# One scale for the whole spatial matrix, from row tiles, in place of one per half from transposed blocks

## The chip, the core and the metric

The kernel runs on one core of a Trainium2 chip. The metric is the device time of one execution in microseconds (us). The kernel before was run three times: 777.92, 780.03 and 781.29 us, with a median of 780.03 us. One further execution was recorded by the hardware profiler; the profile and the trace below are of that one.

A core has five engines that run side by side, each with its own queue of instructions, worked through in order: TensorE (PE, matrix products), VectorE (DVE), ScalarE (ACT), GpSimd (POOL) and SyncE (SP, which here only issues transfers). They wait for one another through semaphores. TensorE writes its results into PSUM, eight banks of [128 x 512] float32; everything else lies in the on-chip memory SBUF, 128 partitions of 207 KB in this kernel, or in device memory.

## The reference

Two blocks follow each other on a sequence of T = 2048 tokens of width D = 1024: a memory-augmented attention with 32 heads, and a gated MLP. The change lies wholly in the second.

```python
def _B_ref(x, w_in, w_sp, b_sp, w_out):     # x: layernorm of h, [1, 2048, 1024]
    z = _gelu(jnp.einsum('bsd,df->bsf', x, w_in))          # w_in [1024, 3584]
    z1 = z[..., :Fh].copy()                                # Fh = 1792
    z2 = _layernorm(z[..., Fh:], axis=-1)
    g = jnp.einsum('ts,bsf->btf', w_sp, z2) + b_sp[None, :, None]   # w_sp [2048, 2048]
    return jnp.einsum('bsf,fd->bsd', z1 * g, w_out)        # w_out [1792, 1024]

h = x + _A_ref(_layernorm(x), ...)
h2 = h + _B_ref(_layernorm(h), ...)
```

All tensors are bfloat16. The spatial matrix `w_sp` mixes tokens: its product with z2 is the gate of z1.

## The kernel before, in words

**A recorder sets the waits.** Each engine's instructions are recorded in the order in which the program issues them. Class `_Recorder` derives the waits from the memory that each instruction reads and writes, in cells of 32 bytes of SBUF and whole banks of PSUM. Each engine then runs its own list in order, so an instruction that waits holds everything behind it on its engine. Since `run` emits every instruction at line 210, the profile gives L210 for nearly all of them, and groups are told apart by the names of their tiles.

**Stages.** First comes the attention (0 to about 310 us), whose output h is written to `out`. Then comes the *z2 half* (to about 404 us): `z2_group(k, tc)` multiplies a row tile of 128 tokens by 448 columns of `w_in` in eight matmuls, and ScalarE's Gelu takes the result from PSUM to `Z2`. There are 4 x 16 such groups, in the order of the list `todo`; a few of them run inside the attention already, and a few output tiles of the attention are mixed in. `z2_stats` and `z2_apply` on VectorE, with two small instructions on GpSimd (`zrs`), normalise the rows into `Z2H` (float16). SyncE loads the column pieces of `w_in` (`win_load`) and transposes the normalised h (`hnT`).

The *z1 half* follows (about 404 to 501 us): for s = 0 to 3 (512 tokens each) and fc = 0 to 13 (128 features each), eight matmuls give a block of z1 transposed, and a Gelu on ScalarE stores it in `Z1T`. Beside it the first half of `w_sp` is prepared.

**The gate in two halves.** The gate is computed for output tokens 0 to 1023 (pr = 0) and then 1024 to 2047 (pr = 1). In each half, `w_sp` is seen as four blocks of 512 x 1024 (`b11`, `b12`, `b21`, `b22`), loaded transposed by SyncE (`sp_load`, four transposing transfers a block), and a Strassen-like scheme uses their sums t1 to t4 and sums of blocks of z2 (`s_sum`, tile `SS`), with seven products of eight matmuls for each of seven groups of features (`gate_group`). The blocks and sums are float16. Since the values of `w_sp` are small, they are first multiplied by a power of two:

```python
def sp_half(pr, k):
    dve.tensor_single_scalar(BH[k][:], RAW[k][:], SC[pr][:], ALU.mult)
```

The power of two comes from the root mean square of the entries: `sp_square` squares half a block on ScalarE and adds up each partition's squares in a column of `SQ` (eight columns), and `sp_scale` copies these to bfloat16 on GpSimd (`SQB`), sums over the partitions with a matmul against a matrix of ones (`ONES`), and makes the scale `SC` and its inverse `INV` in a few tiny instructions on VectorE and one on GpSimd. The inverse is applied in `gate_group`. Scale and inverse exist once for each half pr.

**Between the two gate halves lie the output units.** Each of the 16 units in the loop at line 1110 is a product of 14 matmuls for 128 tokens by 512 columns (`out_unit`); VectorE adds it to the part of h that was loaded back from `out` (`fin`), and ScalarE's queue issues the write. The load of `fin` for unit n + 2 and the write of unit n are both issued from ScalarE's queue, in that order, with four `fin` buffers. While the units run, the second half of `w_sp` is loaded and squared (n = 1 to 8, line 1115), scaled (n = 8, line 1118) and summed (n = 8 to 12), so that the second gate stage can begin. A last stage of 17 output units ends the kernel.

**Banks.** `next_bank` hands out the eight banks of PSUM in turn, in the z2 half, the z1 half, the gate and the output units alike. A group that takes a bank must wait until its previous content was read, eight groups earlier.

**Memory around the change.** `RAW` and `BH` of a block share their place: the scaling is in place. `t3` overwrites `b12`, `t1` takes the place of a dead activation tile. The squares write to a scratch tile `SJ` that nothing reads.

Of the kernel before, what the change touches and what calls it, by code (L numbers as in the profile page):

```python
# [12 lines left out]
T = 2048  # L13
# [245 lines left out]
def bass_sequential_preLN__memory_aug_infini_attn__mixer_gmlp__prompt_kernel(  # L259
# [24 lines left out]
    def tens(name, shape, dt, off):  # L284
        sz = int(np.prod(shape[1:])) * mybir.dt.size(dt)
        assert off % 32 == 0 and off + sz <= ARENA, (name, off, sz)
        t = nc.alloc_sbuf_tensor_at(name, list(shape), dt, offset=abase + off)
        R.space[t[:].tensor.name] = ("sbuf", off)
        return t

    class Bump:
# [4 lines left out]
        def __call__(self, name, shape, dt):  # L296
# [72 lines left out]
          for k, o in ROLES + (("t1", 30), ("t2", 190), ("t3", 22), ("t4", 38))}  # L369
# [4 lines left out]
    ZRS = b3("zrs", [128, NTC], F32)  # L374
    ONES = b3("ones", [128, 128], BF16)
    MHZ = b3("mhz", [128, 1], F32)
    SQ = b3("sq", [128, 8], F32)
    SQB = b3("sqb", [128, 8], BF16)
    TOT = b3("tot", [128, 1], F32)
    TOP = b3("top", [128, 1], F32)  # L380
    SC = [b3("sc%d" % i, [128, 1], F32) for i in range(2)]
    INV = [b3("inv%d" % i, [128, 1], F32) for i in range(2)]
    TMP = {k: tens("tmp_" + k, [128, L], F32, (4 + 2 * i) * K)
           for i, k in enumerate(("s1", "s1b1", "s1b2", "u2", "u3"))}
    SJ = [tens("sj0", [128, 4, L], BF16, 4 * K), tens("sj1", [128, 4, L], BF16, 38 * K)]
    BROW = [tens("brow%d" % i, [128, L], BF16, (132 + i) * K) for i in range(2)]
    WO0 = tens("w_out0", [128, 14, 512], BF16, 118 * K)
    WO1A = tens("w_out1a", [128, 7, 512], BF16, 54 * K)
# [15 lines left out]
    def next_bank():  # L404
        b = rot["banks"][rot["n"] % len(rot["banks"])]
        rot["n"] += 1
        return b
# [390 lines left out]
    def z2_group(k, tc, stage=None):  # L798
        s, tcl = divmod(tc, 4)
        b = next_bank()  # L800
        wi = WIN[k % 3]
        mm8(PS[:, b, 0:448], lambda i: HNT[s][:, i, tcl * 128:(tcl + 1) * 128], lambda i: wi[:, i, 0:448])
        if stage is None:
            z2_gelu(k, tc, PS[:, b, 0:448])
        else:
            act.activation(ZSTG[stage][:], PS[:, b, 0:448], ACTF.Copy)
            staged.append((k, tc, ZSTG[stage][:]))
# [99 lines left out]
    rot["n"] = 0  # L907
    win_load(2)

    todo = [(0, 2), (0, 3), (0, 8), (0, 9), 0, (0, 10), 1, (0, 11), 2, (1, 0), 3]  # L910
    todo += [(1, tc) for tc in range(1, 4)] + [(0, tc) for tc in range(12, NTC)]
    todo += [(1, tc) for tc in range(4, NTC)] + [(k, tc) for k in (2, 3) for tc in range(NTC)]
    for it in todo:
        if isinstance(it, int):
            for half in range(2):
                wo(NSEG - 1, it, half)
                bg_pop()
            continue
        z2_group(*it)
        bg_pop()  # L920
        z2_stats()
        if len(zs) > 1:
            z2_stats()
        if len(zq) > 1:
            z2_apply()
        if it == (0, NTC - 1):
            win_load(3)
        if it == (1, NTC - 1):
            for k in (4, 6, 7):
                win_load(k)  # L930
        if it == (2, NTC - 1):
            win_load(5)
    assert not any(lnq)
    while zs:
        z2_stats()
    pool.memset(ONES[:], 1.0)
    pool.memset(MHZ[:], -0.5)

    def sp_load(pr, k, j):
        r0, c0 = 1024 * pr + (512 if k in ("b12", "b22") else 0), 1024 if k in ("b21", "b22") else 0  # L940
        sp.dma_start_transpose(RAW[k][:, :, j * 128:(j + 1) * 128],
                               B_w_sp[r0 + j * 128:r0 + (j + 1) * 128, c0:c0 + 1024])

    def sp_square(pr, k, h):
        col = 2 * [x for x, _ in ROLES].index(k) + h
        act.activation(SJ[pr][:], RAW[k][:, 4 * h:4 * h + 4, :], ACTF.Square, accum_out=SQ[:, col:col + 1])

    def sp_scale(pr):
        b = next_bank()
        pool.tensor_copy(SQB[:], SQ[:])  # L950
        pe.matmul(PS[:, b, 0:8], ONES[:], SQB[:], start=True, stop=True)
        dve.tensor_reduce(out=TOT[:], in_=PS[:, b, 0:8], axis=mybir.AxisListType.X, op=ALU.add)
        dve.tensor_single_scalar(TOT[:], TOT[:], 1e-30, ALU.max)
        pool.tensor_tensor(TOP[:], TOT[:], MHZ[:], ALU.pow)
        dve.tensor_single_scalar(TOP[:].bitcast(I32), TOP[:].bitcast(I32), 0x7F800000, ALU.bitwise_and)
        dve.tensor_single_scalar(SC[pr][:], TOP[:], 8192.0, ALU.mult)
        dve.reciprocal(INV[pr][:], SC[pr][:])

    def sp_half(pr, k):
        dve.tensor_single_scalar(BH[k][:], RAW[k][:], SC[pr][:], ALU.mult)  # L960

    def sp_sum(o, a, b):
        dve.tensor_tensor(BH[o][:], BH[a][:], BH[b][:], ALU.subtract)
# [25 lines left out]
    def gate_group(pr, g, ba):  # L989
        t1, t2 = slice(1024 * pr, 1024 * pr + 512), slice(1024 * pr + 512, 1024 * pr + 1024)  # L990
        s1, s1b1, s1b2, u2, u3 = (TMP[k][:] for k in ("s1", "s1b1", "s1b2", "u2", "u3"))
        inv = INV[pr][:]

        def stt(o, b, add):
            dve.scalar_tensor_tensor(o, bank(b), inv, add, ALU.mult, ALU.add)

        def out(v, i, t):
            z = Z1T[:, g + 7 * i, t]
            dve.tensor_tensor(z, v, z, ALU.mult)

        act.activation(s1, bank(ba), ACTF.Copy, scale=inv)
        pool.tensor_tensor(s1b2, s1, BROW[1][:], ALU.add)
        pool.tensor_tensor(s1b1, s1, BROW[0][:], ALU.add)
        bb, bc = next_bank(), next_bank()
        prod(bb, SS[:, 1], "t2", True)
        prod(bc, SS[:, 0], "t1", True)
        stt(u2, bb, s1b2)
        if pr == 0 and g == 0:
            sp_sum("t4", "b21", "t2")
        if g < 6:  # L1010
            s_sum(1, g + 1)
        prod(bb, SS[:, 2], "t3", False)
        prod(ba, a_blk(0, 1, g), "b21", False)
        stt(u3, bb, s1b2)
        stt(u3, bc, u3)
        out(u3, 1, t2)
        nb = prod1(g + 1) if g < 6 else None
        if g < 6:
            s_sum(3, g + 1)
        stt(s1, ba, BROW[0][:])  # L1020
        out(s1, 0, t1)
        prod(bc, SS[:, 3], "b22", False)
        if g < 6:
            s_sum(2, g + 1)
        prod(bb, a_blk(1, 1, g), "t4", False)
        stt(u2, bc, u2)
        out(u2, 0, t2)
        if g < 6:
            s_sum(4, g + 1)
        stt(s1b1, bb, s1b1)  # L1030
        out(s1b1, 1, t1)
        return nb
# [28 lines left out]
    for s in range(NSEG):  # L1061
        for fc in range(14):
            k, fl = divmod(fc, 4)
            b = next_bank()
            mm8(bank(b), lambda i: WIZ[k][:, i, fl * 128:(fl + 1) * 128], lambda i: HNT[s][:, i, :])
            act.activation(Z1T[:, fc, s * 512:(s + 1) * 512], bank(b), ACTF.Gelu_apprx_tanh)
            if zq:
                z2_apply()
            if s == 1 and fc in (2, 4, 6, 8):
                sp_square(0, "b11" if fc > 4 else "b21", fc // 2 % 2)  # L1070
            if s == 1 and fc in (10, 12) or s == 2 and fc in (8, 10):
                sp_square(0, "b22" if s == 1 else "b12", fc // 2 % 2)
            if s == 2 and fc == 13:
                sp_scale(0)
            if s == 3:
                if fc < 4:
                    sp_half(0, ("b11", "b12", "b22", "b21")[fc])
                if fc == 4:
                    sp_sum("t1", "b12", "b11")
                if fc == 5:  # L1080
                    s_sum(1, 0)
                    s_sum(2, 0)
                    s_sum(3, 0)
                    s_sum(4, 0)
                if fc == 6:
                    sp_sum("t3", "b22", "b12")
                if fc == 8:
                    sp_sum("t2", "b22", "t1")
        if s == 0:
            for j in range(4):  # L1090
                sp_load(0, "b22", j)
        if s == 1:
            for j in range(4):
                sp_load(0, "b12", j)
            brow_load(0)
# [5 lines left out]
        nb = gate_group(0, g, nb)  # L1101
    fin_load(units[0], act)
    fin_load(units[1], act)
    for k in ("b11", "b21", "b12", "b22"):
        for j in range(4):
            sp_load(1, k, j)
    brow_load(1)
# [2 lines left out]
    for n, u in enumerate(units):  # L1110
        if n + 2 < 16:
            fin_load(units[n + 2], act)
        out_unit(u, (lambda i: WO0[:, i, :]) if u[1] == 0 else
                 (lambda i: WO1A[:, i, :] if i < 7 else WO1B[:, i - 7, :]), act)
        if 0 < n < 9:
            k = (n - 1) // 2
            sp_square(1, ("b11", "b21", "b12", "b22")[k], (n - 1) % 2)
        if n == 8:
            sp_scale(1)
            sp_half(1, "b11")  # L1120
            sp_half(1, "b12")
        if n == 9:
            sp_sum("t1", "b12", "b11")
            sp_half(1, "b22")
        if n == 10:
            sp_sum("t3", "b22", "b12")
        if n == 11:
            sp_sum("t2", "b22", "t1")
        if n == 12:
            sp_half(1, "b21")  # L1130
            sp_sum("t4", "b21", "t2")
        if n == 13:
            for k in range(1, 5):
                s_sum(k, 0)
# [44 lines left out]
```

## Time and profile before

| what | value |
|---|---|
| median of three runs | 780.03 us (777.92 to 781.29) |
| profiled execution | 781.06 us |
| its span, first to last instruction | 779.3 us |
| mean granted TensorE clock | 0.995 |
| PE busy | 765.2 us (98%) |
| DVE busy | 465.6 us (60%) |
| ACT busy | 336.6 us (43%) |
| POOL busy | 201.4 us (26%) |
| read from device memory, written | 34.35 MB, 8.39 MB |
| chain that ended last, by engine | PE 91%, DMA 3%, DVE 3%, ACT 1%, issue 1% |

The page gives each engine's busy time and its share of the span, then the span in 40 equal slices of 19.5 us with one digit each (tenths of busy time; 9 is 90% or more). PEclk is the granted TensorE clock in tenths of full speed. An engine with a share near 100% sets the time; the idle time of the others costs nothing by itself. A list of waits names who released an engine from each wait. The chain that ended last follows the work back from the last instruction, at each step to what released it.

### The profile page before, as it was taken

What the parts mean: (1) busy time and instruction counts of PE and PEld (TensorE: products, weight loads), DVE (VectorE), ACT (ScalarE), POOL (GpSimd) and SP (SyncE); (2) the same over time, 40 slices, a digit from 0 to 9 for tenths busy, and PEclk for the clock granted to TensorE, in tenths of its full rate; (3) what the DMA queues carried; (4) which work ended last, traced back from release to release, by engine and by line L of the source; (5) the groups of instructions that cost most, each with busy time, mean ns of one, the idle gap of its engine ahead of it and who ended that gap; (6) DMA issues with size and microseconds to landing.
All of it is one profiled execution on the core that took longest, in us unless ns stands there. A gap on an engine that the chain in (4) does not pass through costs nothing.

```text
span 779.3 us, 13105 instructions
## 1 busy us (share of the span) xinstructions
PE 765.2 (98%) x5477; PEld 368.4 (47%) x5552; DVE 465.6 (60%) x851; ACT 336.6 (43%) x395; POOL 201.4 (26%) x363
## 2 busy tenths in 40 slices
PE   8999999999999999999999999999999799999998
PEld 4445544555554445455554444444444244444444
DVE  5585689768954775744464004397873386878422
ACT  6777876887778676133333755300002500000000
POOL 2564556555553342100132000112110002112000
PEclk9999999999999999999999999999999899999999
DMA  9654555353425423724311330110039840000122
GB/s 306 162 149 89 95 82 123 82 96 83 101 50 130 105 67 62 202 61 136 96 36 32 55 67 1 55 41 0 1 55 251 161 155 15 1 1 0 61 82 74
DMA packets 131595, 66.66 MB, mean 86 GB/s; under 512 B 95952, under 2 KB 124368, under 8 KB 131536
## 3 DMA queue, kind: packets, MB, share of 16 engines
q1 hardware_dynamic: 124288, 59.01, 32.2%
q10 hardware_dynamic: 7248, 6.82, 3.2%
q8 instruction: 43, 0.70, 0.4%
q14 instruction: 16, 0.13, 0.1%
HBM read 34.35 MB, written 8.39 MB: 55 GB/s over the span
## 4 chain that ended last, share of the span: by engine, by line
PE 91%; DMA 3%; DVE 3%; ACT 1%; issue 1%; ACTq 0%; POOL 0%; DVEq 0%
PE ps L210 91%; DMA out_dram<-fin 2%; DMA wv<-in_A_wv_dram 1%; ACT sj L210 1%; DVE stats L210 1%; ACTq L210 0%; DVE hch L210 0%; DVE pqk L210 0%; DVE otok L210 0%; DVE ta L210 0%; ACT e L210 0%; DVE fin L210 0%; DVE lno L210 0%; ACT L210 0%; DVE rd L210 0%
## 5 line engine op out<-in xcount | busy, mean ns | idle before, releaser
L210 ACT ACTIVATE e<-ps 128x2048 bf16<-128x2048 f32 (+1 forms) x96 | 152.6, 1590 | 41.7 <-PE ps L210 41.5
L210 POOL TENSOR_SCALAR_AFFINE_SELECT e<-e 128x512 bf16<-128x512 bf16 x128 | 90.8, 722 | 131.9 <-ACT e L210 131.9
L210 PE MATMUL ps<-win,hnT 128*128 128x448 bf16 x512 | 98.3, 352 | 0.0
L210 PE MATMUL ps<-hnT,wiz 128*128 128x512 bf16 x439 | 96.2, 379 | 0.5
L210 ACT ACTIVATE tmp_s<-ps,inv 128x512 f32<-128x512 f32 x14 | 9.6, 687 | 159.0 <-DVE z1T L210 131.6
L210 POOL TENSOR_TENSOR tmp_s1b<-tmp_s,brow 128x512 f32<-128x512 f32 x28 | 32.3, 1157 | 168.5 <-ACT tmp_s L210 137.1
L210 PEld LDWEIGHTS ps<-win,hnT 128*128 128x128 bf16 x512 | 49.7, 98 | 46.4 <-issue 0.2
L210 PEld LDWEIGHTS ps<-hnT,wiz 128*128 128x128 bf16 x448 | 43.7, 98 | 52.7
L210 ACT ACTIVATE z<-ps 128x448 bf16<-128x448 f32 x60 | 32.5, 543 | 69.4 <-PE ps L210 69.4
L210 PE MATMUL ps<-xnT,wk 128*128 128x512 bf16 x233 | 59.6, 380 | 1.2
L210 PE MATMUL ps<-wv,xnT 128*128 128x512 bf16 x255 | 59.8, 382 | 0.8 <-DMA wv<-in_A_wv_dram 0.7
L210 DVE TENSOR_TENSOR fin<-fin,ps 128x512 bf16<-128x512 bf16 (+2 forms) x33 | 22.1, 671 | 60.3 <-PE ps L210 42.6
L210 PE MATMUL ps<-wo,oT 128*128 128x512 bf16 x254 | 57.7, 380 | 0.1
L210 DVE BATCH_NORM_STATS2 zst<-z 128x6 f32<-128x448 bf16 x64 | 38.9, 620 | 30.1 <-ACT z L210 30.1
L210 PE MATMUL ps<-xnT,wq 128*128 128x512 bf16 x226 | 54.0, 379 | 1.6
L210 ACT ACTIVATE z1T<-ps 128x512 bf16<-128x512 f32 x56 | 33.4, 596 | 49.1 <-PE ps L210 48.0
L210 PE MATMUL ps<-w_out,z1T 128*128 128x512 bf16 x218 | 49.3, 379 | 0.3
L210 PEld LDWEIGHTS ps<-v,e 128*128 128x128 bf16 x1280 | 38.8, 96 | 14.0 <-issue 6.5
L210 PE MATMUL ps<-v,e 128*128 128x33 bf16 x1280 | 42.2, 178 | 0.0
L210 DVE SCALAR_TENSOR_TENSOR tmp_u<-ps,inv,tmp_s1b 128x512 f32<-128x512 f32 x28 | 21.0, 750 | 31.3 <-PE ps L210 16.7
L210 PEld LDWEIGHTS ps<-wo,oT 128*128 128x128 bf16 x256 | 24.0, 98 | 27.6
L210 PEld LDWEIGHTS ps<-xnT,wk 128*128 128x128 bf16 x256 | 22.6, 98 | 29.9 <-issue 5.0
(143 smaller groups left out, 1108.2 us busy)
## 6 DMA issues: line engine op xcount, KB each, us to landing
xch<-in_A_x_dram SPq DMA_DIRECT2D x16, 256.0 KB, 3.4
xr<-in_A_x_dram SPq DMA_DIRECT2D x16, 256.0 KB, 3.9
out_dram<-hch SPq DMA_DIRECT2D x16, 256.0 KB, 2.4
win<-in_B_w_in_dram SPq DMA_DIRECT2D x4, 896.0 KB, 5.2
wiz<-in_B_w_in_dram SPq DMA_DIRECT2D x3, 1024.0 KB, 5.3
wo<-in_A_wo_dram SPq DMA_DIRECT2D x1, 2048.0 KB, 8.5
fin<-out_dram ACTq DMA_DIRECT2D x16, 128.0 KB, 3.8
out_dram<-fin ACTq DMA_DIRECT2D x16, 128.0 KB, 3.8
```

The source lines that it names most:

```text
L210: ins = getattr(e, op.name)(*op.args, **op.kw)
```

## The change

Scale and inverse are made once, for the whole of `w_sp`, instead of once for each half.

- The squares leave the z1 half and the output units (eight instructions each). In the z2 half, SyncE loads `w_sp` in 16 plain row tiles of [128 x 2048] (`sp_norm_load`) into two buffers `SJ`, and ScalarE squares each in place with the sum in one of 16 columns of `SQ` (`sp_norm`). The first two loads stand after group (0, 12). From group (1, 4) on, the 16 squares are spread over 44 groups; after square r the load of tile r + 2 follows. After the last one GpSimd makes `SQB`.
- `sp_scale` runs once, in the z1 half at s = 0 after fc = 6. It is gone from s = 2, fc = 13 and from output unit 8.
- The scalings and sums of the first half move earlier in the z1 half: `b21`, `b11`, `b22` at s = 2, fc = 6, `b12` at fc = 12; the sums t1 and t3 at s = 3, fc = 0 and 2; `s_sum` at fc = 4. t2 stays at fc = 8.
- Those of the second half are spread over the output units 1 to 10 instead of 8 to 12, each pair of blocks as it comes, and its blocks are loaded in the order `b11`, `b12`, `b22`, `b21`.
- The constant tiles `ONES` and `MHZ` are set ahead of the z2 half.

```diff
+    def sp_norm_load(r):
+        sp.dma_start(SJ[r % 2][:], B_w_sp[r * 128:(r + 1) * 128, :])
+
+    def sp_norm(r):
+        act.activation(SJ[r % 2][:], SJ[r % 2][:], ACTF.Square, accum_out=SQ[:, r:r + 1])
+
+    def sp_scale(b):
+        pe.matmul(PS[:, b, 0:16], ONES[:], SQB[:], start=True, stop=True)
+        dve.tensor_reduce(out=TOT[:], in_=PS[:, b, 0:16], axis=mybir.AxisListType.X, op=ALU.add)
...
         z2_group(*it)
+        if it == (0, 12):
+            sp_norm_load(0)
+            sp_norm_load(1)
+        if it[0] and it[1] > 3 or it[0] > 1:
+            q = 16 * it[0] + it[1] - 20
+            r = (q * 16 + 15) // 44
+            if r < 16 and (q * 16 - 1) // 44 < r:
+                sp_norm(r)
+                if r < 14:
+                    sp_norm_load(r + 2)
+                elif r == 15:
+                    pool.tensor_copy(SQB[:], SQ[:])
         bg_pop()
...
-    def sp_square(pr, k, h):
-        col = 2 * [x for x, _ in ROLES].index(k) + h
-        act.activation(SJ[pr][:], RAW[k][:, 4 * h:4 * h + 4, :], ACTF.Square, accum_out=SQ[:, col:col + 1])
...
-    def sp_scale(pr):
-        b = next_bank()
-        pool.tensor_copy(SQB[:], SQ[:])
-        pe.matmul(PS[:, b, 0:8], ONES[:], SQB[:], start=True, stop=True)
...
-            if s == 1 and fc in (2, 4, 6, 8):
-                sp_square(0, "b11" if fc > 4 else "b21", fc // 2 % 2)
-            if s == 1 and fc in (10, 12) or s == 2 and fc in (8, 10):
-                sp_square(0, "b22" if s == 1 else "b12", fc // 2 % 2)
-            if s == 2 and fc == 13:
-                sp_scale(0)
+            if s == 0 and fc == 6:
+                sp_scale(next_bank())
+            if s == 2 and fc in (6, 12):
+                for k in ("b21", "b11", "b22") if fc == 6 else ("b12",):
+                    sp_half(k)
...
-    for k in ("b11", "b21", "b12", "b22"):
+    for k in ("b11", "b12", "b22", "b21"):
         for j in range(4):
             sp_load(1, k, j)
...
-        if 0 < n < 9:
-            k = (n - 1) // 2
-            sp_square(1, ("b11", "b21", "b12", "b22")[k], (n - 1) % 2)
+        if n == 1:
+            sp_half("b11")
+        if n == 4:
+            sp_half("b12")
+            sp_sum("t1", "b12", "b11")
+        if n == 6:
+            sp_half("b22")
+            sp_sum("t3", "b22", "b12")
         if n == 8:
-            sp_scale(1)
-            sp_half(1, "b11")
-            sp_half(1, "b12")
-        if n == 9:
-            sp_sum("t1", "b12", "b11")
-            sp_half(1, "b22")
+            sp_sum("t2", "b22", "t1")
         if n == 10:
-            sp_sum("t3", "b22", "b12")
-        if n == 11:
-            sp_sum("t2", "b22", "t1")
-        if n == 12:
-            sp_half(1, "b21")
+            sp_half("b21")
             sp_sum("t4", "b21", "t2")
```

More of the change, by code (lines that the diff above doesn't have):

```diff
@@ L376, in bass_sequential_preLN__memory_aug_infini_attn__mixer_gmlp__prompt_kernel @@
     MHZ = b3("mhz", [128, 1], F32)
-    SQ = b3("sq", [128, 8], F32)
-    SQB = b3("sqb", [128, 8], BF16)
+    SQ = b3("sq", [128, 16], F32)
+    SQB = b3("sqb", [128, 16], BF16)
     TOT = b3("tot", [128, 1], F32)
     TOP = b3("top", [128, 1], F32)
-    SC = [b3("sc%d" % i, [128, 1], F32) for i in range(2)]
-    INV = [b3("inv%d" % i, [128, 1], F32) for i in range(2)]
+    SC = b3("sc", [128, 1], F32)
+    INV = b3("inv", [128, 1], F32)
     TMP = {k: tens("tmp_" + k, [128, L], F32, (4 + 2 * i) * K)
            for i, k in enumerate(("s1", "s1b1", "s1b2", "u2", "u3"))}
-    SJ = [tens("sj0", [128, 4, L], BF16, 4 * K), tens("sj1", [128, 4, L], BF16, 38 * K)]
+    SJ = [tens("sj%d" % i, [128, T], BF16, (4 + 4 * i) * K) for i in range(2)]
     BROW = [tens("brow%d" % i, [128, L], BF16, (132 + i) * K) for i in range(2)]
@@ L908, in bass_sequential_preLN__memory_aug_infini_attn__mixer_gmlp__prompt_kernel @@
     win_load(2)
+    pool.memset(ONES[:], 1.0)
+    pool.memset(MHZ[:], -0.5)
+    def sp_norm_load(r):
[5 more added lines that the diff above has]
+        dve.tensor_reduce(out=TOT[:], in_=PS[:, b, 0:16], axis=mybir.AxisListType.X, op=ALU.add)
+        dve.tensor_single_scalar(TOT[:], TOT[:], 1e-30, ALU.max)
+        pool.tensor_tensor(TOP[:], TOT[:], MHZ[:], ALU.pow)
+        dve.tensor_single_scalar(TOP[:].bitcast(I32), TOP[:].bitcast(I32), 0x7F800000, ALU.bitwise_and)
+        dve.tensor_single_scalar(SC[:], TOP[:], 8192.0, ALU.mult)
+        dve.reciprocal(INV[:], SC[:])
     todo = [(0, 2), (0, 3), (0, 8), (0, 9), 0, (0, 10), 1, (0, 11), 2, (1, 0), 3]
@@ L935, in bass_sequential_preLN__memory_aug_infini_attn__mixer_gmlp__prompt_kernel @@
         z2_stats()
-    pool.memset(ONES[:], 1.0)
-    pool.memset(MHZ[:], -0.5)
     def sp_load(pr, k, j):
@@ L942, in sp_load, with sp_half @@
                                B_w_sp[r0 + j * 128:r0 + (j + 1) * 128, c0:c0 + 1024])
-    def sp_square(pr, k, h):
-        col = 2 * [x for x, _ in ROLES].index(k) + h
-        act.activation(SJ[pr][:], RAW[k][:, 4 * h:4 * h + 4, :], ACTF.Square, accum_out=SQ[:, col:col + 1])
-    def sp_scale(pr):
-        b = next_bank()
-        pool.tensor_copy(SQB[:], SQ[:])
-        pe.matmul(PS[:, b, 0:8], ONES[:], SQB[:], start=True, stop=True)
[L952 to L960, printed above, removed]
+    def sp_half(k):
+        dve.tensor_single_scalar(BH[k][:], RAW[k][:], SC[:], ALU.mult)
     def sp_sum(o, a, b):
@@ L991, in gate_group @@
         s1, s1b1, s1b2, u2, u3 = (TMP[k][:] for k in ("s1", "s1b1", "s1b2", "u2", "u3"))
-        inv = INV[pr][:]
+        inv = INV[:]
         def stt(o, b, add):
@@ L1068, in bass_sequential_preLN__memory_aug_infini_attn__mixer_gmlp__prompt_kernel @@
                 z2_apply()
-            if s == 1 and fc in (2, 4, 6, 8):
-                sp_square(0, "b11" if fc > 4 else "b21", fc // 2 % 2)
-            if s == 1 and fc in (10, 12) or s == 2 and fc in (8, 10):
-                sp_square(0, "b22" if s == 1 else "b12", fc // 2 % 2)
-            if s == 2 and fc == 13:
-                sp_scale(0)
+            if s == 0 and fc == 6:
[3 more added lines that the diff above has]
+                    sp_half(k)
             if s == 3:
-                if fc < 4:
-                    sp_half(0, ("b11", "b12", "b22", "b21")[fc])
+                if fc == 0:
+                    sp_sum("t1", "b12", "b11")
                 if fc == 4:
-                    sp_sum("t1", "b12", "b11")
-                if fc == 5:
                     s_sum(1, 0)
@@ L1084, in bass_sequential_preLN__memory_aug_infini_attn__mixer_gmlp__prompt_kernel @@
                     s_sum(4, 0)
-                if fc == 6:
+                if fc == 2:
                     sp_sum("t3", "b22", "b12")
@@ L1114, in bass_sequential_preLN__memory_aug_infini_attn__mixer_gmlp__prompt_kernel @@
                  (lambda i: WO1A[:, i, :] if i < 7 else WO1B[:, i - 7, :]), act)
-        if 0 < n < 9:
-            k = (n - 1) // 2
-            sp_square(1, ("b11", "b21", "b12", "b22")[k], (n - 1) % 2)
-        if n == 8:
-            sp_scale(1)
-            sp_half(1, "b11")
-            sp_half(1, "b12")
-        if n == 9:
-            sp_sum("t1", "b12", "b11")
-            sp_half(1, "b22")
-        if n == 10:
-            sp_sum("t3", "b22", "b12")
-        if n == 11:
-            sp_sum("t2", "b22", "t1")
-        if n == 12:
-            sp_half(1, "b21")
+        if n == 1:
+            sp_half("b11")
+        if n == 4:
+            sp_half("b12")
+            sp_sum("t1", "b12", "b11")
+        if n == 6:
+            sp_half("b22")
+            sp_sum("t3", "b22", "b12")
+        if n == 8:
+            sp_sum("t2", "b22", "t1")
+        if n == 10:
+            sp_half("b21")
             sp_sum("t4", "b21", "t2")
```

## The prediction

> **What bounds the kernel now.** I read the page first: which engine fills the span, and where its row dips. Columns are busy time, share and instructions; then one digit per fortieth (19.5 us) of the span.
>
> ```profile
> PE 765.2 (98%) x5477; PEld 368.4 (47%) x5552; DVE 465.6 (60%) x851; ACT 336.6 (43%) x395; POOL 201.4 (26%) x363
> ...
> PE   8999999999999999999999999999999799999998
> ...
> PEclk9999999999999999999999999999999899999999
> ```
>
> TensorE is the bound. Past its start it dips below 9 in one slice before the end, the 32nd (604 to 624 us), where the granted clock dips too. TensorE's list of waits names the cause (total, times, longest):
>
> ```profile
> PE ps L210 <- POOL sqb L210: 5.3, 1, 5.3
> ```
>
> The chain that ended last, in order of time (start, duration, what), shows what is behind it:
>
> ```profile
> 616.93 0.63 ACT sj L210
> 617.57 1.18 issue
> 618.75 0.20 ACT sj L210
> 619.00 0.20 POOL sqb L210
> 619.25 8.02 PE ps L210 x24
> ```
>
> Squares on ScalarE (`sj`), copied by GpSimd (`sqb`), then TensorE: the `ONES` matmul of `sp_scale(1)`, issued in order after output unit 8, holds units 9 to 15. TensorE's timeline (start, duration, operation, count) gives the price:
>
> ```profile
> 610.75 1.67 PE L210 MATMUL ps<-w_out1a,z1T 128*128 128x512 bf16 x7
> 612.26 1.67 PE L210 MATMUL ps<-w_out1b,z1T 128*128 128x512 bf16 x7
> 619.25 0.19 PE L210 MATMUL ps<-sqb,ones 128*128 128x8 bf16 x1 [5.31 <-POOL sqb L210]
> 619.29 3.15 PE L210 MATMUL ps<-w_out1a,z1T 128*128 128x512 bf16 x7
> 622.24 3.08 PE L210 MATMUL ps<-w_out1b,z1T 128*128 128x512 bf16 x7
> 625.15 1.68 PE L210 MATMUL ps<-w_out1a,z1T 128*128 128x512 bf16 x7
> ```
>
> A unit is 14 matmuls and starts 3.02 us after the last (units 6, 7, 8 start at 604.71, 607.73, 610.75). Unit 9 takes nearly twice that. The stretches say why (the value after POOL is the granted clock):
>
> ```profile
> 586.80:613.90 27.10, 26.99 (x123) 12.12 (x124) 6.92 (x10) 11.45 (x11) 0.00 (x0) 1.00 1.20 240
> 613.90:619.20 5.30, 0.04 (x1) 0.00 (x0) 0.69 (x1) 4.57 (x6) 0.19 (x1) 0.91 0.66 218
> 619.20:625.20 6.00, 5.95 (x16) 2.17 (x17) 3.17 (x7) 0.00 (x0) 0.55 (x1) 0.51 0.00 0
> ```
>
> The idle stretch is followed by 6 us at clock 0.51. Elsewhere the z2 half (289 to 405 us) and the z1 half (405 to 491) show TensorE busy 115.83 of 116.00 and 85.58 of 86.00 us: no gain is to be had there, only loss.
>
> [...] In the z1 half a square stands between two Gelus without a gap:
>
> ```profile
> 434.73 0.60 ACT L210 ACTIVATE z1T<-ps 128x512 bf16<-128x512 f32 x1 [1.13 <-PE ps L210]
> 435.22 1.90 ACT L210 ACTIVATE sj<-b21r 128x2048 bf16<-128x2048 bf16 x1
> 437.02 0.19 ACT L210 ACTIVATION_READ_ACCUMULATOR sj<-b21r 128x1 f32 x1
> 437.11 0.59 ACT L210 ACTIVATE z1T<-ps 128x512 bf16<-128x512 f32 x1
> ```
>
> [...] an output write (`out_dram<-fin`) takes 10.1 us beside transposes and `w_out` loads (chain, 590.52), against a median of 3.8.
>
> **The change, part by part.**
> *Removed, output units:* eight squares (1.906 + 0.19 us each) on ScalarE, and `sp_scale(1)` with its wait. Undisturbed, unit 10 would start at 610.75 + 2 × 3.02 = 616.79; it starts at 625.15. So the wait costs 8.36 us: 5.48 from unit 9's due start (613.77) to the restart, 0.04 for the `ONES` matmul, 2.84 for the slow clock. What is late next? Unit n+8 needs the bank of unit n, that is its `fin` addition on VectorE. Unit 9 needs that of unit 1, done at 593.5; unit 15 (at 631.9) that of unit 7, at 613.5 before. TensorE runs through.
>
> *Moved on VectorE, same stage:* four halvings (1.28 each), four sums (2.28) are spread over n = 1 to 10 instead of 8 to 12. The new wait is VectorE's on the transposes, with `fin` additions behind it, and behind those the writes and `fin` loads on ScalarE's queue. b11 is issued by 578.3 and takes 4 us: there before n = 1 (593). b12 now comes second and replaces t3, last read at about 581.5, so its issue starts some 2 us earlier than b21's (583.24) did; b22 and b21 follow, the last landing as today at about 615. Unit 6 is added at about 610, when b22 (issued by about 601, landing 4 to 8 us) is there; b21 is needed at 620.6. What must be ready: `s_sum` (4 × 0.68) after unit 13 and before the t2 product, 645.01 − 8.36 = 636.65. Unit 13 ends at 628.9, the sums at about 632.5: 4 us of room. The last `fin` load needs the write of unit 11 (about 625.5, 3.5 to 6 us), then 3.8 us: 633 to 635 against unit 15's end at 634.9. That is the tightest place. Behind it wait the write and the first `s1` of ScalarE, hence the gate's products. I take 0; alone it could cost up to about 3 us.
>
> *Added, z2 half:* 16 squares of the same width, in place; price 2.1 us each, from the row above. SyncE issues 16 plain loads of 512 KB. A z2 group takes 1.513 us (Gelus at 376.62, 378.13, ...), 44 groups 66.6 us. ScalarE needs 44 × 0.543 + 16 × 2.1 = 57.5 us of them: 86%. A Gelu comes at most some 2 us later; TensorE has seven other banks, 7 × 1.513 = 10.6 us. So 0. [...]
> *The loads:* 256 KB land in 3.4 us (`xch`), 1024 KB in 5.3 (`wiz`); 512 KB, by the line between them, 4.0. Two buffers: load r+2 follows square r, and two squares lie 5.5 groups = 8.3 us apart, so up to about 6.2 us is hidden. On SyncE's queue the first two loads come after the last hnT transpose (332.0 to 333.2; median landing 3.1), which TensorE needs at about 337.3: up to 1 us if it is slowed, I take 0. Behind the later ones stand `wiz` loads, at about 359.5 instead of 356.9, needed at 405, and b21's transposes, 395 instead of 381.6, now needed at about 466. 0.
>
> *`sp_scale`, once, after z1 group 6 (about 417.5):* its `SQB` copy on GpSimd comes before the zrs of tile 12 (413.1), so about 411.5: 6 us early. VectorE's part stands behind its z2 backlog, which ends at 423.1; its bank is next wanted at about 429.6. It replaces the one at 477: 0. The halvings at s = 2 and 3 have only VectorE's idle time before them (54.8 us before 477.93): 0.
>
> **Sum.** −8.36 us. The profiled execution: 781.06 with a span of 779.3 (1.8 around it), so 772.7, span 770.9. It lies 1.0 above the median of 780.03, so the median becomes **771.7**. The three runs spread over 777.92 to 781.29 (0.43%), hence 0.5% (3.9 us) as the bound of no change.
>
> **Rivals.**
> *Wait in another place (0.12).* VectorE's halvings or late `fin` loads hold the start of the second gate stage. For: the ring of four `fin` buffers already lags TensorE by 4.4 us at unit 2, and the 1792 KB `z1T` load now falls at about 617. Against: 4 us of room. Price 1.5 to 7 us of stall, the upper end with a slow clock again: 773 to 779.
> *Only the idle time is won (0.03).* Another gap triggers the slow clock: 780.03 − 5.5 = 774.5. Against: no other wait of TensorE exceeds 1.3 us.
> *Slower, by late row tiles (0.05).* With landing time L, ScalarE holds the Gelus behind each missing tile; some seven pair cycles lose L − 6.2 each, and past 10.6 us TensorE stops. At 9.4 us (the `w_out1a` load under load) that is 22.4 − 10.6 = 11.8, minus 8.4: 783.5. It decides for slower than now from L = 6.2 + (10.6 + 8.4)/7 = 8.9 us. For: the last `wiz` load took 9.0. Against: DMA share is 0.37 in this stretch, and that one stood behind two others.
> *The change doesn't do what it says (0):* the second `ONES` matmul is gone from the program, and with it anything that could hold TensorE after unit 8 for squares.
>
> **How the numbers follow.** Likeliest, all hidden: 0.80, with its own range 770 to 773.5 (run spread of about 1.5 us). The rest as above. 769.5 to 775.5 holds the likeliest, the clock case and the small end of the first rival. Faster: 0.80 + 0.03 + half of 0.12, rounded to 0.88; same 0.06; slower 0.06 (the row tiles and a sum of mishaps).
>
> **What would show it.** TensorE's list of waits without `sqb`; 9 in the 32nd slice of PE and PEclk; one `ONES` matmul near 417; 16 `sj` squares between 340 and 405 with Gelus at most some 2 us late; unit starts 3.02 apart throughout. I am wrong if TensorE waits on `ps` of ScalarE before 405, or on VectorE near 637.

## The result, and the profile after

The changed kernel takes 772.02 us (median of 771.61 to 772.03, four runs), the kernel before 778.97 us (777.74 to 781.29, four runs): ratio 0.9906, 95% interval 0.9879 to 0.9933. That is 7 us less. Predicted were 771.7 us in a range of 769.5 to 775.5. The profiled execution took 772.03 us with a span of 770.3.

The page of the changed kernel: busy times by engine, then TensorE's busy time and granted clock in 40 slices.

```profile
PE 761.2 (99%) x5476; PEld 367.2 (48%) x5551; DVE 464.5 (60%) x846; ACT 334.2 (43%) x395; POOL 200.0 (26%) x361
...
PE   8999999999999999999999999999999999999998
...
PEclk9999999999999999999999999999999999999999
```

The 7 in the 32nd slice and the 8 in the clock are gone. TensorE's list of waits no longer has `sqb`; what is left is small and in the attention, four waits of 2.4 us in all. The two longest:

```profile
PE ps L210 <- DVE etmp L210: 1.2, 1, 1.2
PE ps L210 <- DMA wv<-in_A_wv_dram: 0.5, 1, 0.5
...
```

TensorE's timeline at the same place, units 8, 9 and the start of 10:

```profile
610.36 1.67 PE L210 MATMUL ps<-w_out1a,z1T 128*128 128x512 bf16 x7
611.87 1.67 PE L210 MATMUL ps<-w_out1b,z1T 128*128 128x512 bf16 x7
613.38 1.67 PE L210 MATMUL ps<-w_out1a,z1T 128*128 128x512 bf16 x7
614.89 1.67 PE L210 MATMUL ps<-w_out1b,z1T 128*128 128x512 bf16 x7
616.40 1.67 PE L210 MATMUL ps<-w_out1a,z1T 128*128 128x512 bf16 x7
```

Unit 10 starts at 616.40 us instead of 625.15. Of these 8.75 us, 8.36 lie between units 8 and 10. The other 0.39 (unit 8 starts at 610.36 instead of 610.75) don't come from the change: they stand already at the beginning of the attention, where the group of matmuls that starts at 26.37 us before starts at 25.99 now. The kernels are alike up to there; in two of those below (the wait taken away, the wait filled) the same group starts at 26.44 and 25.75 us.

### The profile page after: what moved, and what is told of

The parts are those of the page before. It is cut to its first block, busy times and chain, and to the rows that moved or that the text cites. A ratio compares the mean times of both kernels' runs of the same rounds, so it can differ in the third digit from the quotient of the medians.

```text
span 770.3 us, 13128 instructions
## 1 busy us (share of the span) xinstructions
PE 761.2 (99%) x5476; PEld 367.2 (48%) x5551; DVE 464.5 (60%) x846; ACT 334.2 (43%) x395; POOL 200.0 (26%) x361
## 3 DMA queue, kind: packets, MB, share of 16 engines
HBM read 42.74 MB, written 8.39 MB: 66 GB/s over the span
## 4 chain that ended last, share of the span: by engine, by line
PE 93%; DVE 5%; issue 1%; DMA 1%; ACT 0%; DVEq 0%
PE ps L210 93%; DVE stats L210 1%; DMA wv<-in_A_wv_dram 1%; DVE hch L210 1%; DVE otok L210 0%; DVE pqk L210 0%; DVE lno L210 0%; DVE ta L210 0%; DVE etmp L210 0%; DVE rd L210 0%; DVE rdm L210 0%; DVE mv L210 0%; ACT e L210 0%; ACT L210 0%; DVE upd L210 0%
```

## The experiments

The times are compared with the kernel before, run beside them: 779.19 us (775.70 to 782.44, 51 runs) for the first four experiments, 779.1 us (777.88 to 780.65, 10 runs) for the last three. The ratios given are not the quotients of the medians; the two differ by up to 0.0015, why isn't known. The theory: the gain is one wait of TensorE and the slow clock behind it, and everything else in the change is hidden. The rival: it comes from the rest, ScalarE's queue freed of squares or VectorE's work spread out.

### The wait taken away alone

```diff
         if n == 8:
-            sp_scale(1)
             sp_half(1, "b11")
...
-        dve.tensor_single_scalar(BH[k][:], RAW[k][:], SC[pr][:], ALU.mult)
+        dve.tensor_single_scalar(BH[k][:], RAW[k][:], SC[0][:], ALU.mult)
...
-        inv = INV[pr][:]
+        inv = INV[0][:]
```

> The kernel before without its second sp_scale: the second half is scaled with the first half's scale and inverse instead of its own. Its eight squares stay on ScalarE among the output units (their sums go unread), and the scalings and sums on VectorE stay at units 8 to 12. My theory (the whole gain is the wait of TensorE with its slow clock): unit starts 3.02 us apart throughout, 8.3 us less than before, and at most 1 us of that lost again where VectorE's sums end just as the second gate stage wants them: ratio 0.9894 to 0.991. Rival (the gain comes from the squares leaving ScalarE's queue, or from spreading VectorE's work): less than a quarter of it, under 2 us.

Measured: 772.54 us (771.85 to 772.89, five runs), ratio 0.993 (0.9907 to 0.9952). That is above the 0.9894 to 0.991 expected: 0.993 is a gain of some 5.4 us, the medians give 6.7 of the 7.2 us between before and the changed kernel. Even the end of the interval, 0.9952, is a gain of 3.7 us, where the rival had under 2. The eight squares still run among the units and VectorE's work is still at units 8 to 12, so the rival falls. TensorE goes from unit 8 into unit 9 without a stop:

```profile
612.32 1.67 PE L210 MATMUL ps<-w_out1b,z1T 128*128 128x512 bf16 x7
613.83 1.67 PE L210 MATMUL ps<-w_out1a,z1T 128*128 128x512 bf16 x7
```

VectorE's last `s_sum` began at 633.38 us, the t2 product of TensorE at 636.71: the old places were early enough.

### The wait alone, its result unread

```diff
+    def sp_wait():
+        b = next_bank()
+        pool.tensor_copy(SQB[:], SQ[:])
+        pe.matmul(PS[:, b, 0:8], ONES[:], SQB[:], start=True, stop=True)
...
         if n == 8:
+            sp_wait()
             sp_half(1, "b11")
```

The lines come on top of those of the last experiment.

> As e1_no_wait, but with the copy of the sums and the ONES matmul still issued after unit 8, its result read by nobody. It differs from e1_no_wait by one copy on GpSimd and one matmul of 8 columns. My theory: TensorE waits 5.3 to 5.5 us and runs unit 9 at half clock, so within 1 us of the kernel before (ratio 0.999 to 1.001) and 8 us over e1_no_wait. Rival (the matmul only marks a wait that something else would cause anyway, the fin additions for instance): the same as e1_no_wait, within 1 us.

Measured: 779.25 us (777.25 to 781.81), ratio 1.0006 (0.9994 to 1.0018). A matmul of 8 columns that nobody reads, with its copy, costs 779.25 − 772.54 = 6.7 us (8 expected). Its lines in TensorE's timeline:

```profile
619.23 0.19 PE L210 MATMUL ps<-sqb,ones 128*128 128x8 bf16 x1 [5.72 <-POOL sqb L210]
619.27 3.15 PE L210 MATMUL ps<-w_out1a,z1T 128*128 128x512 bf16 x7
622.21 2.78 PE L210 MATMUL ps<-w_out1b,z1T 128*128 128x512 bf16 x7
624.83 1.67 PE L210 MATMUL ps<-w_out1a,z1T 128*128 128x512 bf16 x7
```

The loss is back with these two instructions alone: neither the use of the scale nor anything else of `sp_scale` is needed for it.

### The same wait, one unit later

```diff
         if n == 8:
-            sp_wait()
             sp_half(1, "b11")
...
         if n == 9:
+            sp_wait()
             sp_sum("t1", "b12", "b11")
```

Against the kernel of the last experiment, only the place is another.

> As e2_wait_unread, but with the copy and the unread ONES matmul one unit later, after unit 9 (due to end at 616.8 us in the trace of before, with the squares done at 619.2). My theory: TensorE waits only 2.4 us. If that is too short for the clock to fall, the loss against e1_no_wait is 2.4 us (ratio to before about 0.9925); if the clock falls all the same, it is 2.4 + 2.8 = 5.2 us (ratio about 0.996).

Measured: 777.46 us, ratio 0.9971 (0.9954 to 0.9988), and not one cluster but two: eight runs at 772.54 to 774.19 us, fourteen at 777.12 to 780.05. The median lies 4.9 us over that of the kernel without the wait, near the 5.2 expected for a fallen clock, but it hides the two groups: the middle of the lower one is 1.0 us over (2.4 expected for a full clock), that of the upper one 5.6. The profiled execution (778.66 us) is of the upper group:

```profile
619.91 0.19 PE L210 MATMUL ps<-sqb,ones 128*128 128x8 bf16 x1 [3.19 <-POOL sqb L210]
```

It waited 3.19 us, not 2.4, since in it GpSimd's copy took 1.04 us (618.81 to 619.85) instead of 0.19, and TensorE then ran at a clock of 0.51 for 5.75 us.

### The wait filled with matmuls

```diff
         pool.tensor_copy(SQB[:], SQ[:])
+        for _ in range(26 if pr else 0):
+            pe.matmul(bank(b), ONES[:], WO0[:, 0, :], start=True, stop=True)
```

> The kernel before, with 26 matmuls of ones by 512 columns of w_out into the bank of the second sp_scale, ahead of its ONES matmul; their result is overwritten. 26 x 0.2157 = 5.6 us of work fill the wait. My theory: no wait of TensorE is left to see, but the time until the scale is the same; only the slow clock behind it goes, so 2.8 us less than before (ratio 0.9964), with unit 9 done in 3.02 us. Rival (the slow unit 9 has another cause, such as VectorE or transfers beside it): no change, unit 9 still near 6 us.

Measured: 778.23 us (777.48 to 779.82), ratio 0.9999 (0.9985 to 1.0012): no difference that the measurement shows. In the profiled execution the mechanism is as expected:

```profile
612.92 5.78 PE L210 MATMUL ps<-w_out,ones 128*128 128x512 bf16 x25
618.53 0.17 PE L210 MATMUL ps<-sqb,ones 128*128 128x8 bf16 x1
618.56 1.67 PE L210 MATMUL ps<-w_out1a,z1T 128*128 128x512 bf16 x7
620.07 1.67 PE L210 MATMUL ps<-w_out1b,z1T 128*128 128x512 bf16 x7
```

Unit 9 runs at full speed behind a filled wait (granted clock 1.00 from 618.5 to 633 us), so the slow unit is the clock and not a neighbour. But the 2.8 us didn't come. The filling sets a floor of 5.6 us under the loss (unit 10 starts at 621.58, 5.64 us later than two units after unit 8's start at 609.90), and the first profile of before, with its 8.36 us, would have to be typical for 2.8 us to be saved. By the medians before loses some 7.2 us against the changed kernel, so by this estimate about 1.6 us were to be had; the medians show 1.0, the ratio nothing. How much the slow clock alone costs on average is therefore not shown. That is why the kernel before was profiled again.

### The kernel before, profiled three more times

> The kernel before, unchanged, profiled again. The executions of before spread over 775.7 to 782.4 us, while those of the changed kernel stay within 771.6 to 772.0. My theory: what spreads is the loss at unit 9, of which 8.36 us in the first profile is only one draw: the wait differs by 1 to 2 us with the landing of b22's transposes, and the slow spell behind it by up to 3 us. Time minus this loss (unit 10's start minus unit 8's start minus 6.04 us) is 772 to 773 in every look. Rival (the spread lies elsewhere in the kernel): the loss is 8.4 us in every look and time minus loss differs by as much as the times do.

> As e8_before_look1: another draw of the wait and the slow spell; time minus the loss at unit 9 is again 772 to 773 us.

> As e8_before_look1: another draw of the wait and the slow spell; time minus the loss at unit 9 is again 772 to 773 us.

The loss is unit 10's start minus unit 8's start minus 6.04 us; the slow spell is what the slow clock cost, that is the time from the `ONES` matmul to unit 10, less 3.06. The wait is shown from the modelled end of the matmul before it, so that wait and slow spell together are 0.2 us short of the loss. From 619 to 622 us the granted clock was 0.50 in the second and the third profile and 1.00 in the fourth.

| execution of before | time, us | wait, us | slow spell, us | loss, us | time − loss, us |
|---|---|---|---|---|---|
| the first profile | 781.06 | 5.31 | 2.84 | 8.36 | 772.70 |
| the second | 780.54 | 5.71 | 2.19 | 8.11 | 772.43 |
| the third | 778.51 | 4.06 | 1.69 | 5.95 | 772.56 |
| the fourth | 776.31 | 3.54 | 0.00 | 3.74 | 772.57 |

The times differ by 4.8 us, time minus loss by 0.3. Nearly the whole spread of these four executions sits in this one place, and the changed kernel, which hasn't it, spreads over 0.4 us in four runs. The same difference is 772.26 us for the unread pair (780.73 − 8.47) and 771.84 for the filled wait (777.48 − 5.64), and the kernel without the wait took 772.76 us in its profiled execution. TensorE in the fourth:

```profile
617.31 0.18 PE L210 MATMUL ps<-sqb,ones 128*128 128x8 bf16 x1 [3.54 <-POOL sqb L210]
617.35 1.67 PE L210 MATMUL ps<-w_out1a,z1T 128*128 128x512 bf16 x7
618.85 1.67 PE L210 MATMUL ps<-w_out1b,z1T 128*128 128x512 bf16 x7
620.37 1.67 PE L210 MATMUL ps<-w_out1a,z1T 128*128 128x512 bf16 x7
```

The length of the wait follows the squares, and these in part the transposes of b22: in the second and the fourth profile, ScalarE's first square of b22 waits for the transfer:

```profile
615.03 1.91 ACT L210 ACTIVATE sj<-b22r 128x2048 bf16<-128x2048 bf16 x1 [3.91 <-DMA b22r<-in_B_w_sp_dram]
```

```profile
612.15 1.91 ACT L210 ACTIVATE sj<-b22r 128x2048 bf16<-128x2048 bf16 x1 [1.04 <-DMA b22r<-in_B_w_sp_dram]
```

It starts at 615.03 us in the second and at 612.15 in the fourth. The transposes aren't the only cause: in the first profile this square waited only 0.44 us for them, but the one before it 2.80 us for the landing of a write of `fin`, which the next load of `fin` on the same queue waited for.

### One unit later, profiled again

> The kernel of e3_wait_one_later once more. Its times fell into two groups, 8 of 22 at 772.5 to 774.2 us and 14 at 777.1 to 780.1. My theory: in the lower group the wait is short and the clock stays full, in the upper one the clock falls for 3 to 5 us. So either a time under 774.5 us with a wait under 2.5 us and unit 10 done in 3.02 us, or a time over 777 us with a longer wait and unit 10 above 5 us. Rival (the two groups have nothing to do with the clock): a full clock at 777 us or more, or a fallen one under 774.5.

Measured: 780.39 us. TensorE waited 5.72 us, since here the squares ended only at about 622.3 (one of b11 had waited 5.93 us behind `fin`, and none waited for b22's transposes); the unit behind it took 627.51 − 622.75 = 4.76 us, at a mean clock of 0.63. It is again of the upper group, with a fallen clock as the theory has it, though unit 10 stayed just under the 5 us I had named. No execution of the lower group was profiled; that its clock stayed full shows in the mean granted clock recorded with each run: 1.0 in all eight of the lower group, 0.996 to 0.998 in the fourteen of the upper.

### The cover in the z2 half: squares twice

```diff
         act.activation(SJ[r % 2][:], SJ[r % 2][:], ACTF.Square, accum_out=SQ[:, r:r + 1])
+        act.activation(SJ[r % 2][:], SJ[r % 2][:], ACTF.Square, accum_out=SQX[:])
```

> The changed kernel with each of the 16 row tiles squared a second time in place, its sum going to a column that nobody reads. ScalarE then needs 44 x 0.543 + 32 x 2.05 = 89.5 us in the stretch of 44 groups that TensorE does in 66.6 us. My theory (the squares are free only because ScalarE has room and TensorE has seven more banks, 10.6 us): 89.5 - 66.6 - 10.6 = 12 us over the changed kernel, so about 784 us, ratio to before near 1.006; TensorE waits for ScalarE in pieces under 2 us, and its clock stays full. Rival (ScalarE's load in this half never matters): within 1 us of the changed kernel, ratio 0.991.

`SQX` is a column that nobody reads.

Measured: 782.08 us (781.58 to 782.57), ratio 1.0037 (1.0025 to 1.0048): 10.1 us over the changed kernel, where 12 were expected. TensorE's list of waits:

```profile
PE ps L210 <- ACT z L210: 6.3, 6, 2.6
```

These 6.3 us are less than expected because ScalarE, once behind, takes three waiting Gelus in 1.39 us (0.46 each, not 0.543). But the first of these waits is 2.60 us long, and the clock did fall after it: 0.55 from 383.6 to 387 us. 40 matmuls took 9.43 us instead of some 7.7 (24 take 4.71 at full clock, 16 take 3.20), so 1.7 us more. My expectation of a full clock was wrong; ScalarE had just waited 2.68 us for a row tile (until 379.10), and without that delay it would have been done before TensorE stopped there. The bank cover is as reckoned: TensorE first stopped at 381.0 us, 10.6 us after the end of the group whose Gelu came only at 383.04 (by steps of 1.513 us from the Gelu at 340.20, that group ended at about 370.5).

### The cover in the z2 half: late row tiles

```diff
-        sp.dma_start(SJ[r % 2][:], B_w_sp[r * 128:(r + 1) * 128, :])
+        sp.dma_start(SJ[0][:], B_w_sp[r * 128:(r + 1) * 128, :])
...
-                if r < 14:
-                    sp_norm_load(r + 2)
+                if r < 15:
+                    sp_norm_load(r + 1)
```

`sp_norm` uses the one buffer too, and the second early load is left out.

> The changed kernel with one SJ buffer instead of two: the load of row tile r + 1 is issued only after square r. My theory: a period of square 2.05, issue 0.4 and landing 3.5 us = 6.0 us takes the place of 4.16 us for each tile; 15 x 1.85 = 28 us of lateness, of which TensorE's seven banks hide 10.6: 17 us over the changed kernel, about 789 us, ratio to before near 1.013. Rival (late row tiles are hidden anyway): within 2 us of the changed kernel.

Measured: 787.45 us (786.97 to 788.02), ratio 1.0103 (1.0087 to 1.012): 15.4 us over the changed kernel, where 17 were expected. The lists of waits of TensorE and of ScalarE (330 to 430 us):

```profile
PE ps L210 <- ACT z L210: 11.4, 8, 4.6
```

```profile
ACT sj L210 <- DMA sj<-in_B_w_sp_dram: 40.2, 15, 6.2
```

ScalarE waits 40.2 us for row tiles, TensorE 11.4 us for ScalarE. The expectation had no slow clock, yet some 3 of the 15.4 us are that: after two of the waits 48 matmuls took 10.67 and 10.92 us (clock 0.56 and 0.50 in their first 3.3 us), against some 9.2 at full clock. This is the slower-side rival of the prediction, made real: it is the second buffer that hides the added loads.

### The old order of loads

```diff
-    for k in ("b11", "b12", "b22", "b21"):
+    for k in ("b11", "b21", "b12", "b22"):
```

> The changed kernel with the second half's blocks loaded in the old order b11, b21, b12, b22, while VectorE still wants b12 at unit 4 and b22 at unit 6. My theory: VectorE waits for b12 till about 609 us, some 6 us, and for b22 till about 615; the fin additions behind it come late, TensorE's banks hide that, and the sums end within 2 us of when the second gate stage wants them: 0 to 2 us over the changed kernel, ratio to before 0.990 to 0.993. Rival (the new place of the scalings only works with the new order): 4 us or more over the changed kernel.

Measured: 772.43 us (772.24 to 772.48), ratio 0.991 (0.9894 to 0.9926), 0.4 us over the changed kernel by the medians. VectorE waits for b12 until 605.32 us (609 expected) and for b22 until 612.95 (615 expected), and catches up before the second gate stage: its last `s_sum` starts at 632.79. The new order isn't needed for the gain.

## Why the prediction was right, point by point

**The wait and the clock.** Right in kind and place: one matmul and its copy, put back unread, bring the time back to that of before (ratio 1.0006), and behind the filled wait the clock stays full (1.00).

**Its size.** Here a step was wrong though the sum came out. The 8.36 us are the loss of the profiled execution, whose own sum was 781.06 − 8.36 = 772.70 (772.03 measured; 0.39 of the difference stood already ahead of unit 8). I then subtracted the same 8.36 from the median, as if each execution lost as much. The four profiles of before show 3.74 to 8.36 us. By the medians of the 51 runs and of the changed kernel the typical loss is 779.19 − 772.02 = 7.2 us: the term was 1.2 us too large. That the sum came within 0.4 us all the same was luck: the three runs of before had a median of 780.03, 0.8 us above that of the 51. The spread of before was a sign I read only as noise.

**What is late next in the output units.** Right: TensorE ran through. The last `s_sum` began at 631.65 and ended about 632.3 (predicted 632.5), ahead of the t2 product at 636.26. The "tightest place" was less tight than reckoned: the last `fin` load was issued at 626.85, where the write of unit 11 was to hold it until 629 or later, and the last `fin` addition (634.80) waited for TensorE, not for its load. The order of loads was worth some 0.4 us by the medians, if anything.

**The squares.** 1.90 us each, hidden, and no `ACT_TABLE_LOAD` among them (the only two on ScalarE, of 1.28 us each, start at 0.80 and 300.39 us). But the Gelus were not "at most some 2 us late". I placed the `wiz` loads behind the row tiles' and asked only whether `wiz` would be in time; tile 7, issued after them, shares the transfer engines with 2.5 MB (their busy share from 360 to 373 us was 0.98). It landed after 10.3 us (median of the 16: 3.5, predicted 4.0), and ScalarE's timeline shows it:

```profile
368.66 0.54 ACT L210 ACTIVATE z<-ps 128x448 bf16<-128x448 f32 x1 [0.97 <-PE ps L210]
373.06 1.91 ACT L210 ACTIVATE sj<-sj 128x2048 bf16<-128x2048 bf16 x1 [3.86 <-DMA sj<-in_B_w_sp_dram]
374.88 0.19 ACT L210 ACTIVATION_READ_ACCUMULATOR sj<-sj 128x1 f32 x1
374.97 1.39 ACT L210 ACTIVATE z<-ps 128x448 bf16<-128x448 f32 x3
```

The Gelu due at about 370.2 us started at 374.97, 4.8 us late. Seven other banks cover 10.6 us, so TensorE didn't see it; one late tile is no series of them. Nor did the added reading cost TensorE anything that shows: the kernel reads 42.74 MB instead of 34.35, and the transfer engines' busy share from 289 to 405 us rose from 0.37 to 0.59, with TensorE busy for 115.84 of 116.00 us.

**`sp_scale`, once.** Right: `SQB` at 412.04 us (predicted 411.5), the `ONES` matmul at 416.9 (417.5), VectorE's reduction at 423.69 (423.1). No wait of TensorE.

The changed kernel stays the fastest by its median; taking the wait out alone comes within 0.5 us of it, by medians that weren't measured side by side. In the two profiled executions 0.45 us stand already at the beginning of the attention (25.99 and 26.44 us), where the two kernels are alike.

## What to carry to other kernels

A tiny instruction in the queue of the engine that sets the time can cost as much as the latest of its inputs; make its input long before, or let it stand where the input is there. Before subtracting a stall that one profile shows from a median, look whether the runs spread: this one, which hung in part on transfers, cost 3.74 to 8.36 us in four executions, and taking it away narrowed the spread as well as lowering the time. Work moved to an idle engine is free only by its cover (here each square done twice cost 10.1 us, one buffer instead of two 15.4); count the buffers and banks, and also what the moved transfer itself stands behind.

## What the runs showed of the hardware

The granted clock doesn't follow the length of a wait alone. It stayed at 1.00 after 3.54 us without work (the fourth profile of before) and fell after 3.19 (to 0.51, one unit later), after 2.60 (to 0.55, squares twice) and even after 2.25 us (to 0.50, one buffer). The stretches of the one-buffer kernel, the idle one and the slow one behind it, with the clock after POOL:

```profile
394.70:396.95 2.25, 0.00 (x0) 0.00 (x0) 0.01 (x1) 2.25 (x4) 0.00 (x0) 1.00 0.00 0
396.95:400.30 3.35, 3.34 (x10) 1.34 (x11) 1.67 (x3) 0.97 (x3) 0.00 (x0) 0.50 0.54 161
```

Later in the same execution a slightly longer wait, of 2.34 us, left the clock full; it was 1.00 for the 24 matmuls behind it:

```profile
419.32 5.35 PE L210 MATMUL ps<-hnT,wiz 128*128 128x512 bf16 x24 [2.34 <-ACT z L210]
```

So two waits of nearly the same length ended differently, and the slow spell cost 0 to 2.84 us behind the wait of before in its four profiles. What decides between the two shows in no trace here. In this kernel a wait of 2.25 us was enough to cost the clock.
